# A recurrence with an MLP on one core: N in a second tile ahead of the join, GpSimd's conversions ahead of the third inverse, the first two inverses on ScalarE's queue

## The chip, the cores and the metric

The kernel runs on one core of a Trainium2 chip. The metric is device time in microseconds (us). A timed figure is the median of the fast runs named beside it; a span is the profiled execution alone.

## The reference, cut to what matters

```python
# r, k, v, w, a, b: [4, 8, 768, 40] float32
for t in range(768):
    y[:, :, t] = einsum('bhd,bhde->bhe', r_t, state)
    Sa = einsum('bhde,bhe->bhd', state, a_t)
    state = state * w_t - outer(Sa, b_t) + outer(v_t, k_t)
x = y as [3072, 320]
out = gelu_exact(x @ w_in) @ w_out          # w_in [320, 2048], w_out [2048, 320], float64 inputs
```

The kernel cuts the 768 steps into 12 chunks of 64. In each chunk the recurrence becomes products of small matrices, among them the inverse of a triangular matrix.

## The kernel before

A chunk's inverse is made from N on GpSimd, in two halves of 32 columns. It goes through DRAM (store, fetch), and its off-diagonal block is joined by two rows of small products: `corner` (J from L and N) and `joined` (J2). The other rows of small products are X, RV, A, sap, saT, QY, M, av. One row is 32 calls of `mm` (`make_QY` has two rows); in the trace a row is 64 MATMUL and 64 LDWEIGHTS records, so 128 TensorE instructions. Between the rows, `fill()` puts pieces of the MLP of an earlier chunk: ph (x @ w_in, 4.6 us) and po (gelu @ w_out, 4.5 us).

```python
def store_inverse(c):                       # 2 transfers; fetch_inverse: 6
    ...
        nc.sync.dma_start(out=rows[par], in_=W[par * n:(par + 1) * n])

def corner(c):
    L = work.tile([P, 2 * G * NP, BL], FP32, tag="L", name="L")
    nc.vector.transpose(L, flat(Tt)[:, :, :BL])
    ...                                     # J <- N, L: 64 products
    nc.scalar.copy(Js, J[:, :G * NP])

for c in range(2, NCH):                     # the loop, chunks 2 to 11
    make_X(c); fill()
    ...                                     # loads of chunk n + 1
    make_RV(n); make_sa(c); fill()
    make_saT(c); make_A(n); fill()
    make_y2(c); make_M(c); fill()
    make_QY(c); outputs(c); ...
    make_av(n); sums(n + 1); scale(n + 1); ...; turn_state(); fill()
    store_inverse(n); fetch_inverse(n); turn_b(n + 1); fill()
    corner(n)
    turn_k(n + 1); make_N(n + 1); run(start_inverse(n + 1, nc.gpsimd)); fill()
    joined(n)
```

Ahead of the loop, chunks 0 to 2 are done while the weights arrive as 64-bit words and are converted to float32 on VectorE, ScalarE and GpSimd (ten pieces of w_in on GpSimd, `first_convert`; w_out on VectorE).

## Time and profile before

| | before |
|---|---|
| median of 3 runs | 841.15 us (840.09 to 844.39) |
| profiled span | 838.1 us |
| start: up to X of chunk 2 | 254.34 us |
| from there to the end | 583.8 us, 56.06 us per iteration |
| TensorE busy in that second part | 566.88 us, clock 1.00 |

The second part is nearly full (566.88 of 583.8 us). The start is a chain of waits. A wait is read as "engine, what it was about to compute, whose result ended the wait: us in total, times, longest". The lines are in the prediction.

### The profile page before, as it was taken

The page shows a single profiled execution, that of the slowest core. Times are in us where ns is not written, and L with a number is a line of the kernel's source. Part 1 is how long each engine was busy: PE and PEld are TensorE (multiplying, and loading weights), DVE is VectorE, ACT ScalarE, POOL GpSimd, SP SyncE. Part 2 cuts the span into 40 slices and gives each one's busy share as a digit, 9 for nine tenths or more (in the row PEclk, how much of TensorE's full clock was granted, in tenths as well). Part 3 has the DMA queues.
Part 4 walks back from the last instruction along what each step waited for, and adds up shares of the span by engine and source line. Part 5 has one row for each costly group of instructions (what it writes and reads, how often), then busy time and mean ns, then how long its engine had stood idle before and what let it go on. Part 6 is the DMA issues. An engine that isn't in the chain of part 4 may idle for free.

```text
span 838.1 us, 30219 instructions
## 1 busy us (share of the span) xinstructions
PE 702.7 (84%) x13646; PEld 563.3 (67%) x13646; DVE 279.1 (33%) x422; ACT 214.0 (26%) x260; POOL 315.2 (38%) x781
## 2 busy tenths in 40 slices
PE   7236771165669999999999999999999999999997
PEld 4226661054448878778788787787887877868785
DVE  3763440147542422432424324324233243211000
ACT  5002540212312412422323124223232242111010
POOL 4282336620105507418246074182461751810000
PEclk8555595575859999999999999999999999999999
DMA  9876743017617247354372473543724733020000
GB/s 132 158 156 130 147 112 89 0 40 155 142 34 140 43 82 130 60 103 80 64 135 50 84 135 55 109 77 68 129 57 76 142 55 65 4 53 10 25 9 16
DMA packets 274705, 70.27 MB, mean 84 GB/s; under 512 B 263248, under 2 KB 267856, under 8 KB 274576
## 3 DMA queue, kind: packets, MB, share of 16 engines
q1 hardware_dynamic: 274412, 68.17, 42.6%
q8 instruction: 107, 1.75, 0.9%
q14 instruction: 22, 0.18, 0.1%
q10 hardware_dynamic: 164, 0.16, 0.1%
HBM read 54.13 MB, written 10.22 MB: 77 GB/s over the span
## 4 chain that ended last, share of the span: by engine, by line
PE 73%; POOL 6%; DMA 6%; issue 5%; SPq 4%; DVE 4%; ACT 0%; POOLq 0%; DVEq 0%
PE ph L726 25%; PE po L734 24%; PE QY L100 5%; PE J L100 2%; PE N_ps L100 2%; DMA w_out_sb<-in_moe_w_in_dram 2%; PE cum L100 2%; PE M_ps L100 1%; POOL W L548 1%; POOL mant L281 1%; PE sap L100 1%; POOL tmp L546 1%; PE saT_ps L100 1%; PE X L100 1%; PE wT_ps L100 1%
## 5 line engine op out<-in xcount | busy, mean ns | idle before, releaser
L726 PE MATMUL ph<-xt,w_in_sb 64*128 64x256 f32 x1920 | 225.8, 388 | 42.2 <-ACT gt L728 29.8
L734 PE MATMUL po<-w_out_sb,gt 128*128 128x320 f32 x768 | 225.7, 448 | 9.1 <-DVE w_out_sb L277 8.0
L726 PEld LDWEIGHTS ph<-xt,w_in_sb 64*128 64x128 f32 x1920 | 185.7, 190 | 68.0 <-ACT gt L728 30.2
L734 PEld LDWEIGHTS po<-w_out_sb,gt 128*128 128x128 f32 x768 | 145.9, 195 | 72.2 <-DVE w_out_sb L277 12.4
L546 POOL TENSOR_TENSOR tmp<-W,Nb 128x126 f32<-128x126 f32 (+22 forms) x310 | 111.8, 361 | 213.2 <-DMA Nb<-N 189.7
L548 POOL TENSOR_TENSOR W<-W,tmp 128x126 f32<-128x126 f32 (+22 forms) x310 | 113.9, 368 | 24.3
L728 ACT ACTIVATE gt<-ph 128x1024 f32<-128x1024 f32 x48 | 49.1, 1024 | 232.5 <-PE ph L726 197.5
L738 DVE COPY os<-po 128x320 f32<-128x320 f32 x24 | 11.8, 492 | 152.5 <-PE po L734 152.5
L413 POOL TENSOR_TENSOR ks<-k_raw,part 128x640 f32<-128x640 f32 x10 | 21.2, 2119 | 100.5 <-ACT part L378 85.1
L100 PE MATMUL RV_ps<-rT,vT 40*64 40x64 f32 x768 | 16.4, 244 | 30.8 <-DVE rT L166 30.8
L100 PEld LDWEIGHTS RV_ps<-rT,vT 40*64 40x64 f32 x768 | 14.7, 156 | 34.5 <-issue 34.5
L686 DVE TENSOR_TENSOR xt<-QY,wpT 128x512 f32<-128x512 f32 x24 | 15.5, 686 | 65.5 <-PE QY L100 65.5
L464 DVE TENSOR_TENSOR SM<-M_ps,upper 128x1024 f32<-128x1024 f32 x12 | 14.7, 1224 | 65.7 <-PE M_ps L100 65.7
L464 DVE TENSOR_TENSOR A<-A_ps,upper 128x1024 f32<-128x1024 f32 x12 | 14.7, 1221 | 54.6 <-PE A_ps L100 54.6
L520 ACT COPY avs<-av 128x640 f32<-128x640 f32 x12 | 8.3, 692 | 90.4 <-PE av L100 51.8
L464 DVE TENSOR_TENSOR VR<-RV_ps,upper 128x1024 f32<-128x1024 f32 x12 | 14.7, 1225 | 47.7 <-PE RV_ps L100 47.7
L100 PE MATMUL J<-L,N 32*32 32x32 f32 x768 | 9.9, 204 | 23.9 <-DVE L L585 23.9
L270 ACT ACTIVATE power<-power,rebias 128x320 uint32<-128x320 uint32 (+1 forms) x26 | 16.0, 623 | 51.6 <-DVE power L269 51.6
L100 PEld LDWEIGHTS J<-L,N 32*32 32x32 f32 x768 | 8.9, 116 | 29.4 <-issue 29.4
L464 DVE TENSOR_TENSOR N<-N_ps,upper 128x1024 f32<-128x1024 f32 x12 | 14.7, 1225 | 36.0 <-PE N_ps L100 36.0
L424 DVE TENSOR_TENSOR aT<-aT,wpT 128x1024 f32<-128x1024 f32 x12 | 24.0, 2001 | 1.6 <-ACT wpT L380 0.4
L728 ACT ACT_TABLE_LOAD x10 | 12.8, 1283 | 42.6 <-PE ph L726 40.1
(133 smaller groups left out, 869.0 us busy)
## 6 DMA issues: line engine op xcount, KB each, us to landing
Nb<-N SPq DMA_DIRECT2D x22, 256.0 KB
VR<-in_v_dram SPq DMA_DIRECT2D x24, 160.0 KB
out_dram<-os SPq DMA_DIRECT2D x48, 80.0 KB
w_tile<-in_w_dram SPq DMA_DIRECT2D x22, 160.0 KB
b_raw<-in_b_dram SPq DMA_DIRECT2D x22, 160.0 KB
k_raw<-in_k_dram SPq DMA_DIRECT2D x22, 160.0 KB
v_pairs<-in_v_dram SPq DMA_DIRECT2D x48, 72.0 KB
r_pairs<-in_r_dram SPq DMA_DIRECT2D x48, 72.0 KB
```

The source lines that it names most:

```text
L100: nc.tensor.matmul(o, lhsT, rhs, start=first, stop=True, skip_group_check=True)
L270: nc.scalar.activation(power, power, ACT.Relu, bias=rebias, scale=8.0)
L413: nc.gpsimd.tensor_tensor(ks[:, :, :, :D], raws.pop((c, "k")), rwv, ALU.mult)
L424: nc.vector.tensor_tensor(flat_a, flat_a, wp, ALU.mult)
L464: nc.vector.tensor_tensor(to, pt, upper.unsqueeze(1).to_broadcast([P, 2 * G * NP, C]), ALU.mult)
L546: eng.tensor_tensor(t, W[:, :rows, j:j + 1].to_broadcast([P, rows, rest]), Nb[:, j:j + 1, j + 1:].to_broadcast([P, rows, rest]), ALU.mult)
L548: eng.tensor_tensor(W[:, :rows, j + 1:], W[:, :rows, j + 1:], t, ALU.add)
L686: nc.vector.tensor_tensor(xt[:, :NP, g * P:(g + 1) * P].rearrange("p i (e t) -> p i e t", e=2), Y, wp[:, g, :, :, :C], ALU.mult)
L726: nc.tensor.matmul(ph[:, x, s], w_in_sb[half(x), kt, p * P:(p + 1) * P], xt[half(x), kt], start=kt == 0, stop=kt == NK - 1)
L728: nc.scalar.activation(gt[:, 4 * q:4 * q + 4].rearrange("p (x s) t -> p x s t", x=2), ph, ACT.Gelu)
L734: nc.tensor.matmul(po[:, g], gt[:, f, g * P:(g + 1) * P], w_out_sb[:, f], start=f == 0, stop=f == NF - 1)
L738: nc.vector.tensor_copy(os, po[:, g])
```

## The change

Three intents: the first inverses should not queue behind SyncE's loads; GpSimd's conversions should not wait behind the third inverse; and N of the chunk after next, in a second tile, should no longer wait for the corner, so that the join can move behind X. Its core:

```diff
-        N = t["N"] = work.tile(..., tag="turned" if c == 1 else "N", name="N")
+        if c > 1 and c % 2:
+            N = work.tile([P, 4 * DM], FP32, tag="spare", name="N")[:, :2 * G * NP * C]
+        else:
+            N = work.tile(..., tag="turned" if c == 1 else "N", name="N")
...
-    def store_inverse(c):
+    def store_inverse(c, eng=nc.sync):      # fetch_inverse alike
...                                          # the start
-    first_load(True, 0, early(4))
     run(inverse)
-    store_inverse(0)
     turn_v(0)
     turn_r(0)
+    store_inverse(0, nc.scalar)
+    load_VR(1)
+    fetch_inverse(0, nc.scalar)
...
+    store_inverse(1, nc.scalar)
...
+    fetch_inverse(1, nc.scalar)
...
     make_N(2)
+    convert(3, True)
     run(start_inverse(2, nc.gpsimd))
...                                          # the loop, n2 = c + 2
+        corner(c)
         make_X(c)
         fill()
         if more2:
-            load_next(n + 1)
+            load_next(n2)
+        joined(c)
         if more:
             make_RV(n)
+            make_A(n)
+        fill()
         make_sa(c)
-        fill()
         make_saT(c)
-        if more:
-            make_A(n)
         fill()
...
-        if more:
-            corner(n)
         if more2:
-            turn_k(n + 1)
-            make_N(n + 1)
-            run(start_inverse(n + 1, nc.gpsimd))
+            make_N(n2)
+            run(start_inverse(n2, nc.gpsimd))
+            turn_k(n2)
         fill()
-        if more:
-            joined(n)
```

More of the change, by code (lines that the diff above doesn't have):

```diff
@@ L203 @@
     ahead = {n: t.rearrange("p (g h d) -> p g h d", g=G, h=H) for n, t in ahead.items()}
-    spare_raw = const.tile([P, 4 * DM], UINT32, name="spare_raw")
+    spare_raw = work.tile([P, 4 * DM], UINT32, tag="spare", name="spare_raw")
     early_a = spare_raw.bitcast(FP32).rearrange("p (n d) -> p n d", d=BW)
@@ L487, in make_N @@
         t = turned_in[c]
-        N = t["N"] = work.tile([P, 2, G, NP, C], FP32, tag="turned" if c == 1 else "N", name="N")
+        if c > 1 and c % 2:
+            N = work.tile([P, 4 * DM], FP32, tag="spare", name="N")[:, :2 * G * NP * C]
+            N = N.rearrange("p (j g n t) -> p j g n t", j=2, g=G, n=NP)
+        else:
+            N = work.tile([P, 2, G, NP, C], FP32, tag="turned" if c == 1 else "N", name="N")
+        t["N"] = N
         masked(flat(N), products("N_ps", t["nT"], t["aT"], True))
@@ L559, in store_inverse, with fetch_inverse @@
         for par in range(2):
-            nc.sync.dma_start(out=rows[par], in_=W[par * n:(par + 1) * n])
+            eng.dma_start(out=rows[par], in_=W[par * n:(par + 1) * n])
         stored[c] = inv
-    def fetch_inverse(c):
+    def fetch_inverse(c, eng=nc.sync):
         inv = stored.pop(c)
@@ L569, in fetch_inverse @@
                 at = j * HP + z * BL
-                nc.sync.dma_start(out=flat(Tt)[at:at + BL, :, z * BL:(z + 1) * BL],
+                eng.dma_start(out=flat(Tt)[at:at + BL, :, z * BL:(z + 1) * BL],
                                   in_=inv[j, z].rearrange("n s t -> s n t"))
         for j in range(2):
-            nc.sync.dma_start(out=T2[j * HP:j * HP + BL], in_=inv[j, 1].rearrange("(n z) s t -> z s n t", z=2)[1])
+            eng.dma_start(out=T2[j * HP:j * HP + BL], in_=inv[j, 1].rearrange("(n z) s t -> z s n t", z=2)[1])
         inverses[c] = Tt, T2
@@ L812 @@
     first_load(False, 1)
-    first_load(True, 0, early(4))
     run(inverse)
-    store_inverse(0)
     turn_v(0)
     turn_r(0)
+    store_inverse(0, nc.scalar)
+    load_VR(1)
+    fetch_inverse(0, nc.scalar)
+    first_load(True, 0, early(4))
+    load_v(1)
     mask_A(0)
@@ L821 @@
     turn_k(1)
+    corner(0)
     make_A(1, False)
-    load_VR(1)
-    fetch_inverse(0)
-    load_v(1)
-    first_load(False, 2, early(5, 4))
-    first_pieces(range(NK), 0, nc.gpsimd)
+    joined(0)
     mask_A(1)
-    corner(0)
-    joined(0)
     make_X(0)
     make_sa(0)
-    convert(1)
-    store_inverse(1)
+    make_saT(0)
+    first_pieces(range(NK), 0, nc.gpsimd)
+    store_inverse(1, nc.scalar)
     nc.gpsimd.memset(spare_st.rearrange("p e i g d -> p (e i g) d")[:, :, D:], 0.0)
     load_r(1)
-    load_w(2)
-    make_saT(0)
     convert(1)
-    fetch_inverse(1)
     make_y2(0)
     make_M(0)
-    convert(1)
+    fetch_inverse(1, nc.scalar)
+    load_w(2)
     load_a(2)
     load_kb(2)
-    logs(2)
-    first_load(False, 3)
+    first_load(False, 2, early(5, 4))
+    convert(2)
     make_QY(0)
@@ L850 @@
     pieces.append(mlp(0))
+    first_load(False, 3)
     first_load(True, 1, spare_raw[:, :LW])
@@ L860 @@
     make_X(1)
+    logs(2)
     convert(1)
@@ L866 @@
     make_sa(1)
-    scale(2)
+    scale_b(2)
     turn_a(2)
     scale_a(2)
+    make_saT(1)
     convert(1)
-    make_saT(1)
     turn_b(2)
+    scale_k(2)
     convert(1)
@@ L877 @@
     make_N(2)
+    convert(3, True)
     run(start_inverse(2, nc.gpsimd))
-    convert(1)
+    second_load(4, 6)
+    second_load(5, 2, spare_raw)
+    second_load(6, 0, spare_raw)
     fill()
+    second_pieces((*range(NF - 2), NF - 1, NF - 2), nc.vector)
     make_y2(1)
     make_M(1)
-    convert(1)
+    seconds(2, (7, 14))
+    fill()
     load_v(2)
     load_r(2)
-    turn_k(2)
-    convert(1, True)
-    second_load(4, 6)
-    fill()
-    second_pieces((*range(NF - 2), NF - 1, NF - 2), nc.vector)
-    seconds(2, (5, 2, spare_raw), (6, 0, spare_raw))
-    fill()
     make_QY(1)
     outputs(1)
+    pieces.append(mlp(1))
+    seconds(2, (8, 12), (9, 10))
     load_VR(3)
-    pieces.append(mlp(1))
-    seconds(3, (7, 14), (8, 12))
-    load_w(3)
-    load_a(3)
-    load_kb(3)
+    fill()
+    turn_k(2)
     turn_v(2)
@@ L905 @@
     make_A(2)
+    load_w(3)
+    load_a(3)
+    load_kb(3)
+    seconds(3)
+    seconds(2, (10, 2, spare_raw), (11, 0, spare_raw), (12, 14))
+    fill()
     make_av(2)
-    seconds(2, (9, 10))
+    logs(3)
     load_v(3)
     load_r(3)
-    seconds(2, (10, 2, spare_raw), (11, 0, spare_raw))
-    fill()
-    logs(3)
-    seconds(2, (12, 14))
     sums(3)
-    store_inverse(2)
-    fetch_inverse(2)
     scale(3)
@@ L919 @@
     scale_a(3)
-    seconds(2, (13, 2, spare_raw), (14, 0, spare_raw))
+    seconds(2)
     turn_state()
     fill()
-    seconds(1, (15, 14))
+    seconds(2, (13, 2, spare_raw))
+    store_inverse(2)
+    fetch_inverse(2)
     turn_b(3)
+    seconds(1, (14, 0, spare_raw), (15, 14))
     seconds(2, last=True)
     fill()
-    corner(2)
-    turns_b(3)
     make_N(3)
     run(start_inverse(3, nc.gpsimd))
+    turns_b(3)
     fill()
-    joined(2)
     for c in range(2, NCH):
-        n = c + 1
-        more, more2 = n < NCH, n + 1 < NCH
+        n, n2 = c + 1, c + 2
+        more, more2 = n < NCH, n2 < NCH
+        corner(c)
         make_X(c)
@@ L939 @@
         if more2:
-            load_next(n + 1)
+            load_next(n2)
+        joined(c)
         if more:
             make_RV(n)
+            make_A(n)
+        fill()
         make_sa(c)
-        fill()
         make_saT(c)
-        if more:
-            make_A(n)
         fill()
@@ L952 @@
         if more2:
-            logs(n + 1)
+            logs(n2)
         make_QY(c)
@@ L957 @@
         if more2:
-            load_VR(n + 1)
-            turn_a(n + 1)
-            turn_v(n + 1)
-            turn_r(n + 1)
+            load_VR(n2)
+            turn_a(n2)
+            turn_v(n2)
+            turn_r(n2)
         fill()
@@ L965 @@
         if more2:
-            sums(n + 1)
-            scale(n + 1)
-            scale_a(n + 1)
+            sums(n2)
+            scale(n2)
+            scale_a(n2)
         if more:
@@ L975 @@
         if more2:
-            turn_b(n + 1)
+            turn_b(n2)
         fill()
-        if more:
-            corner(n)
         if more2:
-            turn_k(n + 1)
-            make_N(n + 1)
-            run(start_inverse(n + 1, nc.gpsimd))
+            make_N(n2)
+            run(start_inverse(n2, nc.gpsimd))
+            turn_k(n2)
         fill()
-        if more:
-            joined(n)
     fill(1000)
```

## The prediction

> **What bounds the kernel now.** I read the engine totals first, then the slices, then a table of stretches, then TensorE's waits, and last the timeline around the longest wait. The slices say where time is lost:
>
> ```profile
> PE   7236771165669999999999999999999999999997
> ...
> POOL 4282336620105507418246074182461751810000
> ...
> PEclk8555595575859999999999999999999999999999
> ```
>
> One slice is 21 us. TensorE is full from slice 13 on; before that it is half empty and mostly at a lowered clock, and slices 7 and 8 are nearly empty. The stretches put numbers on it (us busy and instructions per engine, granted clock, DMA share, GB/s):
>
> ```profile
> 105.00:127.50 22.50, 16.45 (x336) 14.08 (x327) 10.19 (x15) 9.57 (x14) 7.02 (x8) 0.92 0.45 119
> 127.50:159.60 32.10, 1.81 (x8) 1.41 (x8) 0.45 (x1) 1.02 (x1) 24.47 (x64) 0.51 0.21 48
> 159.60:185.00 25.40, 16.44 (x208) 12.33 (x208) 8.64 (x16) 8.49 (x13) 7.84 (x7) 0.68 0.08 27
> 185.00:254.34 69.34, 43.52 (x540) 29.69 (x540) 42.48 (x91) 16.45 (x24) 2.90 (x4) 0.68 0.49 105
> 254.34:838.00 583.66, 566.88 (x11088) 458.23 (x11080) 165.37 (x193) 146.29 (x166) 227.22 (x590) 1.00 0.40 74
> ```
>
> 254.34 us is where X of chunk 2, the loop's first product, starts. After it TensorE works 567 of 584 us at full clock: only less work could shorten that part. Before it lie 254 us that are a chain of waits. The longest, from TensorE's waits between 105 and 165 us, and its cause in the timeline:
>
> ```profile
> PE ph L726 <- ACT gt L728: 29.8, 1, 29.8
> ```
> ```profile
> 157.05 0.23 POOL L548 TENSOR_TENSOR W<-W,tmp 128x16 f32<-128x16 f32 x1
> 157.23 1.27 POOL L281 TENSOR_TENSOR mant<-mant,gt 128x512 f32<-128x512 f32 x1
> 158.54 1.02 ACT L728 ACTIVATE gt<-ph 128x1024 f32<-128x1024 f32 x1 [34.95 <-POOL mant L281]
> ...
> 159.61 2.08 PE L726 MATMUL ph<-xt,w_in_sb 64*128 64x256 f32 x8 [29.80 <-ACT gt L728]
> ```
>
> "ACT gt" is not the cause. The activation writes gt where raw words of w_in still lie, GpSimd's conversion (L281) must read those first, and GpSimd has done nothing but the third inverse since 130.3 us. The inverse holds the conversion, that the activation, that the PSUM buffer, that TensorE.
>
> [...] Here the first inverse is done at 49.2 us, but its store stands behind eight loads on the sync queue and is issued at 55.55; 6.3 us is all that ScalarE's queue can save there. [...] the 64 instructions of N_ps take 1.16 us in the loop (clock 1.00) and 1.98 us in the start, and the clock in the long wait is 0.51. So an estimate for the start must use the start's own durations. [...] The trace has 1.28 us for the load[...], so I count 1.28.
>
> **The change, part by part.** The number of instructions of each kind hardly changes (ten conversions on GpSimd, sixteen on VectorE, eleven inverses on GpSimd, one on VectorE); order and queues do. I followed each engine's new instruction order by hand with durations of the trace.
>
> *1. The first two inverses on ScalarE's queue.* Before:
>
> ```profile
> 43.85 11.60 SPq L325 DMA_DIRECT2D w_out_sb<-in_moe_w_in_dram  x8
> ...
> 55.55 1.97 SPq L560 DMA_DIRECT2D inv<-W  x2
> ...
> 62.90 0.71 DVE L585 STREAM_TRANSPOSE L<-Tt 128x512 f32<-128x512 f32 x1 [2.23 <-DMA Tt<-inv]
> ```
>
> After: issued at about 50, in competition with the w_in loads landed at 55 to 56, fetched by 59 to 60; L some 3.5 us earlier, and sap at about 64.5 instead of 67.8. But these issues and their waits now stand in ScalarE's program ahead of its arithmetic. The second inverse is stored after saT (about 70), landed at about 75, fetched by 77 to 79; only then can ScalarE do its part of the first conversion, so GpSimd starts it at about 79.5 to 80.5 (78.8 before). xt comes at about 83.5 (82.8). Logs(2), now after av, put an Ln with its table load (2 us) between av and cum. The fifth conversion, which the first ph waits for, starts at about 113.5 and is written at 116 (114.3). Sum of part 1: early gain given back, **+1 to +2 us** at 116.
>
> *2. Conversions ahead of the third inverse.* One conversion takes a period of 5.0 us on the ring of DVE, ScalarE and GpSimd (starts before: 157.2, 162.2, 167.2). After: ks(2) 116 to 117.6; second-half conversions start at about 118.6, 125.7 (ScalarE waits for the end of the first ph and loads its table), 130.7, 135.6, and the last, overlapped, at 138.2, ending at **140.8** (before 172.4: 31.6 earlier). TensorE does both first ph, N and M until about 129, idles until 139 to 141, then the rest of the third ph, QY (3 us) and the fourth ph: end at about **152**, against 181.4 for the fourth ph and 184.3 for QY before: 32 us earlier. The idle of 30 becomes one of 10 to 12.
>
> *3. The third inverse later.* It starts at 141 instead of 130 and ends after its 27 us at about **168**. It is needed only by the store ahead of chunk 2, at 216.5 us before and about 190 in the new order. It lies beside other work.
>
> *4. Second weights and the join.* From RV(2) the order of work is much as before: before, RV(2) starts at 195.5, last conversion ends at 238.6, X(2) starts at 254.3, 58.8 us in all. After: outputs(1) on VectorE to 151, two conversions (1.93 us each), two transposes, RV(2) at about 157, masks to 162, five conversions to 172; then av, Ln, cum, Exp, nb, aT (12 us in which VectorE converts nothing), from 184 four conversions to 192; store and fetch of the inverse to 197; the loads of the last two pieces behind it on the sync queue, landed at 201; last conversion ends at 206.5 to 209. Then the rest of po (2 us), N and kT (3.9), po (6.4, as at 247.3 before, clock recovering), os, L and J (2.5): X(2) at **221 to 224**, 30 to 33 us earlier. (The length from RV(2) is then 64 to 67, some 6 us more than before: the corner comes later, and the last two loads wait for the fetch.)
>
> *5. N ahead of the join, second tile.* N(c+2) no longer waits for the corner to have read N(c+1). But in the loop GpSimd has slack (it waits 179.5 us in all for Nb), and TensorE's only loop wait stays:
>
> ```profile
> 357.23 0.49 DVE L738 COPY os<-po 128x320 f32<-128x320 f32 x1 [6.22 <-PE po L734]
> 357.64 0.70 DVE L585 STREAM_TRANSPOSE L<-Tt 128x512 f32<-128x512 f32 x1
> ...
> 358.49 0.74 PE L100 MATMUL J<-L,N 32*32 32x32 f32 x64 [1.29 <-DVE L L585]
> ```
>
> In the new order L again follows an os on VectorE, and J again follows that po on TensorE: 1.29 us per chunk as before. The second ph of a chunk now needs the first's activation: its end comes 2.4 us after ph (ph ends 316.0, activation 318.47), while J2, RV and A fill 2.8 us. Just enough. An iteration stays at 56.06 us. From X(2) to the end: 583.7 plus one join (0.7) that moved behind X: 584.4.
>
> **Sum.** 221 to 224 plus 584.4 is 805 to 808.5 us of span; the timed median lies 3 us above the profiled span (841.15 against 838.1): 808 to 811.5. I take **810 us**.
>
> **Rivals.** (a) ScalarE's queue hurts: if the inverse's small pieces (64 KB writes in rows of 128 bytes) get half of the DMA engines, ScalarE's arithmetic waits longer, each us of it in the conversions' path. The DMA share is 0.70 between 50 and 105 us, so 5 to 8 us are possible: 815 to 818. (b) The second weights bind, not the inverse: VectorE is busy 42.5 of the 69 us from 185 on, and the sync queue carries the last loads behind the inverse; if a spare half comes free late, the gain shrinks by 5 to 10: 815 to 820. If those loads land early, X(2) could come at 216: 803. (c) The loop: if J's wait vanished, 9 times 1.29, 11.6 us more gain, 798; if ph waited for the activation (table load included), up to 1 us per chunk, 820. For (c) I see nothing in the order that removes the wait. (d) The stall merely moves: TensorE waits for the late inverse instead. Against it speaks 168 versus about 190.
>
> **Range and chances.** My errors are sums of hand-followed waits, some 6 us either way, wider on the slow side for contention: 799 to 822 should hold it 8 times in 10. The limit of 2% faster is 824.3: faster 0.95, same 0.04, slower 0.01.
>
> **What would show it.** Right: GpSimd's ten conversions end near 141 and the inverse's columns run 142 to 169; the wait of 29.8 is gone with some 10 us of waits for w_in_sb in its place; X(2) starts at 221 to 224; iterations stay at 56.06 with 1.29 us before each J; first L near 59.5, yet the first conversion no earlier than 79. Wrong: X(2) after 232 or before 215, a loop iteration off by over 0.5 us, or TensorE waiting for L because the third inverse was fetched late.

## The result

The changed kernel takes **856.07 us** (median of 4 runs, 854.54 to 857.22) against 842.77 (4 runs, 840.09 to 845.93) of the kernel before on the same chip: ratio 1.0155, 95% interval 1.0112 to 1.0199, so slower, but by less than 2%. Ratios are the mean time of one kernel's fast runs over that of the other's of the same rounds, so they are not quite the ratio of the medians. 810 was predicted, with a range of 799 to 822. The span is 855.5 us.

The slices of the profile after, one digit for each of 40 equal slices of the span, for TensorE, GpSimd and TensorE's granted clock:

```profile
PE   6206366647489989989999999899899999999997
POOL 4381224771036146154173182361541832700000
PEclk9556677766688989999999999999999999999999
```

The hole of slices 7 and 8 has gone, but TensorE is no fuller than before in slices 1 to 12, and in the loop some slices now show 8. The table of stretches (us, then busy us and instructions of TensorE, its weight loads, VectorE, ScalarE, GpSimd; clock; DMA share; GB/s) puts both losses into numbers:

```profile
183.90:245.05 61.15, 41.30 (x477) 26.53 (x477) 34.45 (x74) 15.29 (x21) 9.10 (x22) 0.68 0.51 99
245.05:855.50 610.45, 582.62 (x11152) 470.31 (x11144) 165.26 (x193) 145.68 (x167) 224.38 (x590) 0.97 0.37 70
```

X of chunk 2 starts at 245.05 us: 9.3 us earlier than before, where some 30 to 33 were predicted. From there the kernel needs 610.45 us instead of 583.8, where 584.4 were predicted. Two separate losses, then.

**The start.** TensorE's waits between 30 and 255 us, after:

```profile
PE RV_ps L100 <- DVE rT L166: 40.6, 2, 29.8
PE po L740 <- DVE w_out_sb L277: 15.7, 9, 6.9
PE J L100 <- DVE L L591: 15.2, 2, 14.0
PE ph L732 <- POOL w_in_sb L282: 9.3, 1, 9.3
```

The same view of the kernel before has this for RV:

```profile
PE RV_ps L100 <- DVE rT L166: 30.8, 2, 19.7
```

The wait of 29.8 us for ScalarE's gt has shrunk to one of 9.0 (not among the lines above), and a wait of 9.3 us for w_in_sb has come, where some 10 us for w_in_sb alone were predicted. But RV of chunk 0 now waits 10 us longer for rT, the transposed r, and J waits 14.0 us for L. The timeline shows where r was (start, us it took to issue, SyncE's queue), before:

```profile
34.74 4.34 SPq L158 DMA_DIRECT2D r_pairs<-in_r_dram  x8
```

and after:

```profile
35.37 23.39 SPq L158 DMA_DIRECT2D r_pairs<-in_r_dram  x8
...
61.00 1.25 DVE L166 STREAM_TRANSPOSE rT<-r_pairs 128x1024 f32<-128x1024 f32 x1 [10.07 <-DMA r_pairs<-in_r_dram]
```

The waits of SyncE's queue name what it stood for:

```profile
SPq L158 <- DMA Tt<-inv: 19.7, 2, 18.7
```

A load of r waited 18.7 us until the first inverse had been fetched, with which it has nothing to do in the program. Everything behind it on SyncE's queue came late.

**The loop.** TensorE's waits between 255 and 760 us, after:

```profile
PE J L100 <- DVE L L591: 10.4, 8, 1.3
PE A_ps L100 <- issue: 10.3, 8, 2.4
```

The kernel before has in the same window only its J wait:

```profile
PE J L100 <- DVE L L585: 11.6, 9, 1.3
```

"issue" is time in which nothing that the profile shows held the engine. The timeline of one iteration, after, around such a place:

```profile
312.55 1.16 PE L100 MATMUL RV_ps<-rT,vT 40*64 40x64 f32 x64
313.53 0.52 PE L100 MATMUL A_ps<-aT,kT 40*64 40x64 f32 x23
316.45 1.35 PE L100 MATMUL A_ps<-aT,kT 40*64 40x64 f32 x41 [2.40 <-issue]
317.73 6.90 PE L732 MATMUL ph<-xt,w_in_sb 64*128 64x256 f32 x40
```

A_ps stops after 23 of its 64 products, although the program has a wait only in front of the first. And the ph behind it takes 6.90 us instead of 4.59: the clock granted is 0.50 from 315.63 to 322.45 us, 0.66 on average over this ph, where it is 1.00 over the whole loop of the kernel before. The iterations (X to X) last 61.23, 61.36, 59.16, 58.94, 58.14, 59.42, 57.22 and 56.88 us instead of 56.06.

### The profile page after: what moved, and what is told of

The parts are those of the page before. It is cut to its first block, busy times and chain, and to the rows that moved or that the text cites.

```text
span 855.5 us, 30268 instructions
## 1 busy us (share of the span) xinstructions
PE 710.2 (83%) x13646; PEld 569.0 (67%) x13646; DVE 283.1 (33%) x422; ACT 213.7 (25%) x260; POOL 314.7 (37%) x781
## 3 DMA queue, kind: packets, MB, share of 16 engines
q8 instruction: 107, 1.75, 0.9%
## 4 chain that ended last, share of the span: by engine, by line
PE 70%; issue 10%; SPq 5%; DVE 5%; DMA 4%; POOL 4%; ACT 1%; ACTq 0%; POOLq 0%; DVEq 0%
PE ph L732 25%; PE po L740 22%; PE QY L100 5%; PE J L100 2%; PE A_ps L100 2%; SPq L158 2%; PE RV_ps L100 2%; PE cum L100 1%; PE sap L100 1%; PE N_ps L100 1%; PE saT_ps L100 1%; POOL mant L281 1%; PE X L100 1%; PE wT_ps L100 1%; PE kT_ps L388 1%
## 5 line engine op out<-in xcount | busy, mean ns | idle before, releaser
L732 PE MATMUL ph<-xt,w_in_sb 64*128 64x256 f32 x1920 | 236.4, 402 | 18.4 <-POOL w_in_sb L282 9.3
L740 PE MATMUL po<-w_out_sb,gt 128*128 128x320 f32 x768 | 223.9, 444 | 17.4 <-DVE w_out_sb L277 15.7
L732 PEld LDWEIGHTS ph<-xt,w_in_sb 64*128 64x128 f32 x1920 | 194.7, 199 | 45.3 <-POOL w_in_sb L282 9.9
L740 PEld LDWEIGHTS po<-w_out_sb,gt 128*128 128x128 f32 x768 | 144.0, 193 | 80.9 <-DVE w_out_sb L277 22.8
L614 DVE COPY Tt<-J 32x512 f32<-32x512 f32 x12 | 8.3, 689 | 75.6 <-ACT Tt L614 75.6
L100 PE MATMUL A_ps<-aT,kT 40*64 40x64 f32 x768 | 19.2, 249 | 15.3 <-issue 13.8
L100 PEld LDWEIGHTS A_ps<-aT,kT 40*64 40x64 f32 x768 | 16.8, 160 | 17.0 <-issue 14.9
L442 ACT COPY kT<-kT_ps 128x1024 f32<-128x1024 f32 x12 | 12.1, 1012 | 58.7 <-PE kT_ps L388 58.7
L641 DVE COPY SM<-sap 128x640 f32<-128x640 f32 x12 | 9.9, 825 | 50.6 <-PE sap L100 50.6
```

The costliest lines, as they stand in the source:

```text
L100: nc.tensor.matmul(o, lhsT, rhs, start=first, stop=True, skip_group_check=True)
L442: nc.scalar.copy(kT, flip(by_pair(t["ks"]), "kT_ps"))
L732: nc.tensor.matmul(ph[:, x, s], w_in_sb[half(x), kt, p * P:(p + 1) * P], xt[half(x), kt], start=kt == 0, stop=kt == NK - 1)
L740: nc.tensor.matmul(po[:, g], gt[:, f, g * P:(g + 1) * P], w_out_sb[:, f], start=f == 0, stop=f == NF - 1)
```

## The experiments

In the diffs, "start" is everything ahead of the loop. Sixteen kernels ran in four batches; all were correct. The kernel before took 843.29, 840.83, 841.06 and 841.11 us (medians of 7) beside them.

### Taking the two losses apart

**sync**: the changed kernel, with the first two inverses back on SyncE's queue.

```diff
-    store_inverse(0, nc.scalar)
+    store_inverse(0)
-    fetch_inverse(0, nc.scalar)
+    fetch_inverse(0)
...                                  # the same for inverse 1
```

> The changed kernel with the first two inverses back on SyncE's queue; everything else of the change stays. Theory: the start's loss comes from the two queues sharing completion semaphores, so that r_pairs' load waited on SyncE's queue for the inverse's fetch. Then r_pairs is issued in 4 to 5 us instead of 23.4, RV of chunk 0 starts near 52 instead of 62, the conversions on GpSimd end near 141 to 146 instead of 161, X of chunk 2 starts at 221 to 228 instead of 245, and the loop stays as slow as in the changed kernel (610 us from X of chunk 2 to the end): 831 to 840 us in all, 16 to 24 below the changed kernel. Rival: the order of the conversions and the second weights ate the start's gain, the queue is innocent; then X of chunk 2 stays at 240 or later and the total at 850 or more.

Measured: 837.93 us, ratio 0.9915 (0.9866 to 0.9965). The loads of r and X of chunk 2, in its timeline:

```profile
33.99 4.52 SPq L158 DMA_DIRECT2D r_pairs<-in_r_dram  x8
...
226.88 1.14 PE L100 MATMUL X<-st,aT 40*64 40x40 f32 x64
```

The theory holds: RV of chunk 0 starts at 51.8 us; GpSimd's last conversion starts its second step at 138.9 us and takes 1.27, so it ends at 140.2, just ahead of the 141 to 146 expected; and the loop stays slow (839.7 minus 226.88 is 612.8 us).

**loopb**: the changed kernel with the loop of before; `corner(2)` and `joined(2)` are back at the end of the start.

```diff
-        corner(c)
         make_X(c)
...                                  # all of the loop's part of the change undone
```

> The changed kernel with the loop of the kernel before (one tile order for N, the corner and the join at the end of an iteration); the start stays as changed, ScalarE's queue included. Theory: the order of the loop, not the start or the second tile, costs the 26 us after X of chunk 2. Then X of chunk 2 stays near 245, the iterations are 56.1 us again, no stall in the middle of A_ps, and the total is 829 to 835. Rival: the loop lost its time to something that the start left behind (a clock, the state of the tiles); then it stays at 850 or more.

Measured: 833.14 us (0.9875; 0.9831 to 0.992). X of chunk 2 stays at 244.97, seven of its eight full iterations last 56.06 us (the other 57.65), and A_ps does not stall. The theory holds.

**startb**: the start of before, the second tile for N, the changed loop.

```diff
-    store_inverse(0, nc.scalar)
...                                  # all of the start's part of the change undone
```

> The kernel before with only the loop changed (second tile for N, N ahead of the join, the products in the changed order); its start and its queues are those of before. Theory: the loop's order alone costs 25 to 27 us: X of chunk 2 at 254 to 256, A_ps stalls of 1 to 2.5 us in the middle of its products in the early iterations, total 864 to 872, 3% slower than before. Rival: the loop's loss comes from the changed start; then this is 838 to 845.

Measured: 865.3 us (1.0249; 1.0202 to 1.0296). X of chunk 2 came at 249.1, a little earlier than I expected; A_ps stalls seven times. The changed loop alone is slower.

**sync_loopb**: both undone.

> The changed start with the inverses on SyncE's queue, and the loop of the kernel before. Theory: both losses are gone and the gain that was predicted for the start (30 us) appears: X of chunk 2 at 221 to 228, iterations of 56.1 us, total 806 to 816. Rival (the start's gain is eaten by the second weights): X of chunk 2 at 240 or later, total 826 or more.

Measured: 815.51 us (0.9665; 0.9617 to 0.9712), X of chunk 2 at 231.56, later than the 221 to 228 expected and 4.7 us later than in `sync`. The join of chunk 2 (0.7 us) stands ahead of X here and behind it in `sync`; the rest is not explained and may be scatter between executions: `before` and `before_A`, whose starts are the same, have this X at 254.34 and 259.76. Differences of some 5 us in one profile's start are therefore not read as effects. With both losses out, the time is 5.5 us above the 810 that was predicted for the whole change.

### The start: how one queue held the other

**act0** keeps only the first inverse on ScalarE's queue, **act1** only the second.

```diff
 act0:                                   act1:
-    store_inverse(1, nc.scalar)         -    store_inverse(0, nc.scalar)
+    store_inverse(1)                    +    store_inverse(0)
...                                      # fetch_inverse alike
```

> The changed kernel with only the first inverse's store and fetch on ScalarE's queue; the second is back on SyncE's. Theory of shared completion semaphores: the load of r_pairs, built between the two, still has to wait for that inverse's fetch: issued over about 23 us as in the changed kernel, X of chunk 2 near 243 to 247, total 850 to 858. Rival: the second inverse (or the load on ScalarE's program) did the harm: then r_pairs takes 4 to 5 us and the total is 833 to 842.

> The changed kernel with only the second inverse's store and fetch on ScalarE's queue; the first is back on SyncE's. Theory of shared completion semaphores: the load of r_pairs has its plain turn of semaphores again and is issued in 4 to 5 us, X of chunk 2 at 225 to 232, total 833 to 842. Rival: any use of ScalarE's queue costs as much: total 850 or more.

Measured: act0 851.87 us (1.0109; 1.0051 to 1.0167), act1 837.4 (0.9977; 0.9905 to 1.0049). The loads of r in act0's timeline:

```profile
34.34 23.51 SPq L158 DMA_DIRECT2D r_pairs<-in_r_dram  x8
```

and in act1's:

```profile
35.96 4.49 SPq L158 DMA_DIRECT2D r_pairs<-in_r_dram  x8
```

It is the first inverse that costs most, not the use of ScalarE's queue as such. X of chunk 2 comes at 239.5 in act0 (I had expected 243 to 247) and at 229.2 in act1. The second inverse holds SyncE's queue too, at less cost: in the changed kernel a load of w_in waits 8.4 us for its store,

```profile
SPq L325 <- DMA inv<-st: 8.4, 1, 8.4
```

and in act1 a load of v waits 6.0 us for it:

```profile
SPq L158 <- DMA inv<-st: 7.9, 2, 6.0
```

The trace records with each transfer which semaphore it waits for and which it counts up. In the changed kernel (times on the page's clock):

```
35.37  SyncE    r_pairs, 1st of 8   waits for S109   counts up S109
36.00  SyncE    r_pairs, 2nd        waits for S101   counts up S101
53.34  ScalarE  Tt<-inv, 1st of 4   waits for S99    counts up S106
55.20  SyncE    r_pairs, 3rd        waits for S106   counts up S106
```

Eight semaphores (101 and 104 to 110) serve the transfers of both queues in turn. The third load of r is to use S106 after the inverse's fetch, so it waits until that has landed: the fetch's last update of S106 is at 55.18 us, r is issued at 55.20. In `sync`, `act1` and the kernel before, the eight loads of r use 105 to 110, 101, 104 in plain turn, and no transfer of the inverse stands between them. The trace gives the number as an operand of the transfer's instruction. In the changed kernel the numbers fit one turn over both queues merged: eight loads of v with the inverse's two stores among them, then the last two loads of N, Tt, r and T2 mixed (105 N, 106 Tt, 107 N, 108 Tt, 109 r, 110 Tt, 101 r, 104 Tt, 105 T2, 106 r). This is not the order of the program, where the loads of r stand ahead of the inverse's store and fetch (so act0's "built between the two" is not right for the loads of chunk 0). Why the turn runs so is not shown.

### The loop: what stops A_ps

The first theory was that three rows of small products behind one another (J2, RV, A: 384 instructions) outrun TensorE's instruction stream.

**startb_rv**: RV out of that place.

```diff
-            make_RV(n)
             make_A(n)
...
             turn_b(n2)
+            make_RV(n2)
```

> The kernel of run startb (start of before, changed loop) with RV of the next chunk moved from between J2 and A_ps to just ahead of N, so that no three runs of small products stand behind one another. Theory: the stall in A_ps is TensorE's instruction stream not coming fast enough[...]. Then the stall is gone, the iterations are 56 to 57 us, and the total is 838 to 848. Rival: A_ps stalls for another reason (its operands, a DMA); then it still stalls and the total stays at 858 or more.

**startb_loads**: the loads elsewhere.

```diff
-        if more2:
-            load_next(n2)
         joined(c)
...
         make_saT(c)
+        if more2:
+            load_next(n2)
```

> The kernel of run startb with the loads of the chunk after next moved from before J2 to after saT; J2, RV and A_ps stay in a row. Theory (instruction stream): stalls and total stay, 858 to 870. Rival: the loads collide with the J2, RV, A stretch and make the stall; then the stall is gone and the total falls to 838 to 848.

**before_A**: in the kernel before, A moved behind RV, so that RV, A and sap stand in a row. (The expectation names J2; in fact X and ph stand between J2 and RV there.)

```diff
             make_RV(n)
+            make_A(n)
...
-        if more:
-            make_A(n)
```

> The kernel before with one move: A_ps of the next chunk right behind RV in the loop, as in the changed kernel, and nothing else of the change. Now J2, RV and A_ps stand in a row. Theory (instruction stream): stalls in A_ps appear here too, each some 2 us with a lowered clock behind it, 2 to 3 us per iteration in all; total 855 to 870. Rival: the cost lies in N ahead of the join or in the second tile; then this stays at 840 to 846.

Measured: startb_rv 864.69 us (1.0254; 1.0189 to 1.0319), startb_loads 867.6 (1.0327; 1.0276 to 1.0379), before_A 843.89 (1.0022; 0.9981 to 1.0064). The loads are innocent. But the theory fell in this form: startb_rv still stalled, now inside ph, three times (5.1 us in the profile, which is of the fastest of its four executions), and before_A has three rows in a row without any stall.

The next theory came out of the raw trace. The page of the changed kernel lists a queue of instructions whose count fits TensorE's (packets, MB, share of the DMA engines):

```profile
q8 instruction: 107, 1.75, 0.9%
```

1.75 MB over 107 is 16384 bytes a packet. The kernel has 27,481 TensorE records: 107 blocks of 256 are 27,392, so the count fits one packet for 256 instructions. Numbering TensorE's records by their start, from 0, every stall falls on the same number modulo 256:

```
changed kernel, stalls after X of chunk 2
instruction   modulo 256   stopped   packet landed before it goes on
 5569         193          2.12 us   1.64 us
 7873         193          2.40      1.29
10177         193          1.30      1.40
12481         193          1.08      1.55
14785         193          0.33      1.26
17089         193          1.58      1.72
19393         193          0.87      1.67
21697         193          0.67      1.37
```

In the eighteen kernels there are 92 such stalls of over 0.25 us after X of chunk 2, all at 193 modulo 256, each 1.2 to 1.8 us after a packet has landed; the other gaps there are waits for semaphores, at any number. In the second part of the kernel before, the packets start between 4.6 us ahead of and 2.2 us behind such a number, one packet for each. The reading that fits: 193 is a block's edge, and TensorE stops there when the next block has come too late. The next two runs move the edges without touching the order.

**sync_64** and **sync_256**: tiny products in the warm-up at the very start, results unread.

```diff
         mm(pt[:, n % 2], w_in_sb[:, 0, :P], w_in_sb[:, 0, :512])
+    for n in range(32):                 # sync_256: 128
+        mm(pt[:BL, 0, :BL], w_in_sb[:BL, 0, :BL], w_in_sb[:BL, 0, BL:2 * BL])
```

> Run sync with 32 tiny products (64 TensorE instructions, results unread) added right at the start of the program, where TensorE is idle; nothing else. In the runs so far every stall in the loop falls on a TensorE instruction whose number is 193 modulo 256, 1.2 to 1.8 us after a packet of the instruction queue has landed. Theory: instructions come in blocks of 256, and the stall depends on where the block boundary falls, not on the order as such. 64 more instructions move the boundary from A_ps back into RV, with the boundary before it in ph. Then the stalls vanish or shrink below 0.5 us, iterations are near 56.1 us, total 810 to 818. Rival: the row J2, RV, A_ps as such is too dense, or A_ps waits for data; then 32 dummies change nothing: 833 to 842.

> The control of run sync_64: 128 tiny products, 256 TensorE instructions, one whole block. Theory: the boundary is back in A_ps, the stalls are back as in run sync (0.5 to 2.5 us each, at 193 modulo 256 again): total 833 to 842. Rival: the dummies act in another way (a warmer clock at the start, a shift in time); then this is like run sync_64 or better.

Measured: sync_64 842.92 us (1.0002; 0.994 to 1.0064), sync_256 847.61 (1.0077; 1.0019 to 1.0135). The first is a miss in two ways. Each tiny product is four TensorE instructions, not two (27,611 records against 27,483), so the shift was 128 and not 64; and the stalls did not vanish: eight of nine moved out of A_ps (two into X, two into the ph behind X, four into the ph behind A), still at 193 modulo 256. sync_256 shifted by 512, two whole blocks, and the stalls are back in A_ps in eight of nine cases. It is slower than `sync` because its X of chunk 2 comes at 235.1 instead of 226.9: the longer warm-up delayed the start (RV of chunk 0 starts at 61.2 us instead of 51.8).

With that, the question became whether the changed order is worse in itself or only met the edges badly. **beforeA_p128** and **before_p128** put the same 32 products (128 instructions) into before_A and into the kernel before; **sync_p64** puts 16 (64 instructions) into `sync`; **fill_p128** is told further down.

> Run before_A (RV, A and sap in a row, no stall at 843.9 us) with 32 tiny products, 128 TensorE instructions, at the start. If the phase decides: the boundary moves from A_ps + 57 to RV + 57, the block behind it is RV's rest, A and the head of sap, 2.0 us of work, and sap stalls by 1 to 2.5 us in every iteration: 858 to 872 us. If the order as such decides (J2 ahead of RV and A): no stalls, 840 to 848.

> The kernel before with the same 128 instructions at the start. Its densest rows are two runs of products (256 instructions) with ph or po between them. If two in a row are safe in most phases: no stall over 1 us, 839 to 849. If the kernel before was only lucky in its phase: stalls as in run sync, 855 or more.

> Run sync with 16 tiny products, 64 TensorE instructions. The boundaries move from A_ps + 42 to RV + 106, from J2 + 42 to the last fifth of ph, from X + 3 to the middle of J. If the phase decides alone, this is the best one for the changed loop that I find: stalls near 1 us in RV or A or none, total 815 to 832. If the changed order is too dense in any phase: stalls of over 1.5 us somewhere in each iteration, 833 or more.

Measured: beforeA_p128 877.57 us (median of 3 fast runs, a fourth was slow; 1.0414, 1.0339 to 1.049), before_p128 846.93 (1.0075; 1.0027 to 1.0122), sync_p64 835.41 (0.9948; 0.9908 to 0.9988). Two of these are misses in size: beforeA_p128 is slower than the 858 to 872 expected, and sync_p64 lies above its 815 to 832, with stalls of 0.5 to 1.7 us. before_A's timeline has the row without a gap:

```profile
321.41 1.16 PE L100 MATMUL RV_ps<-rT,vT 40*64 40x64 f32 x64
322.39 1.11 PE L100 MATMUL A_ps<-aT,kT 40*64 40x64 f32 x64
323.33 1.09 PE L100 MATMUL sap<-part,Tt 64*64 64x40 f32 x64
324.35 4.59 PE L726 MATMUL ph<-xt,w_in_sb 64*128 64x256 f32 x40
```

In beforeA_p128 the same row stops inside sap, where it was expected:

```profile
321.20 1.16 PE L100 MATMUL RV_ps<-rT,vT 40*64 40x64 f32 x64
322.18 1.11 PE L100 MATMUL A_ps<-aT,kT 40*64 40x64 f32 x64
323.11 0.63 PE L100 MATMUL sap<-part,Tt 64*64 64x40 f32 x29
325.68 1.28 PE L100 MATMUL sap<-part,Tt 64*64 64x40 f32 x35 [1.94 <-issue]
326.90 7.18 PE L726 MATMUL ph<-xt,w_in_sb 64*128 64x256 f32 x40
```

128 unread instructions at the start cost 34 us here: nine stalls of 19.3 us together, and the clock, at half for 27.3 us around them. So the place of the edges decided whether this dense row stalled. But order matters too. In the kernel before, where never more than two rows stand together, the same shift brings six stalls of 3.5 us in all. In the changed loop none of the four phases (places of the edges) tried is free of stalls (8.8 us in `sync`, 14.8, 10.2 and 8.4 us in sync_64, sync_256 and sync_p64).

### A version that beats both

**sync_fill**: sync_loopb, with L transposed first and N and kT of the chunk after next (second tile) put ahead of J in one run. RV and A stay apart, as before.

```diff
         if more:
-            corner(n)
+            turn_L(n)                   # the transpose of L alone
         if more2:
-            turn_k(n + 1)
             make_N(n + 1)
             run(start_inverse(n + 1, nc.gpsimd))
+            turn_k(n + 1)
+        if more:
+            corner(n)
         fill()
```

> The start of run sync_loopb, and the loop of before with N of the chunk after next ahead of J in the same run (second tile) and L transposed first, and RV and A apart as before. Theory: N and kT fill J's wait of 1.29 us per iteration and no stall appears: iterations near 55 us, 8 to 12 us below sync_loopb (815.5), total 803 to 809. Rival: the wait moves to another place in the loop or a stall appears; then it stays at 813 or more.

> Run sync_fill with the same 128 instructions at the start. If its rows of products are short enough in any phase: 803 to 812. If it was lucky: stalls of 1 to 3 us per iteration and 820 or more.

Measured: sync_fill **805.68 us** (0.9566; 0.953 to 0.9602), fill_p128 807.06 (0.9597; 0.9569 to 0.9625). J no longer waits in sync_fill's loop:

```profile
332.27 1.16 PE L100 MATMUL N_ps<-aT,nT 40*64 40x64 f32 x64
333.36 1.09 PE L388 MATMUL kT_ps<-ident,ks 128*128 128x128 f32 x8
334.38 0.75 PE L100 MATMUL J<-L,N 32*32 32x32 f32 x64
```

Six of its eight full iterations last 54.71 us, 1.35 less than 56.06. One stall of 0.4 us appears when the edges are shifted by 128, so the time holds in both phases tried. This is where the second tile pays: N has to stand *in front of J, in the same run*, while VectorE does L.

## Why the prediction was wrong, point by point

1. **"+1 to +2 us" for the first two inverses on ScalarE's queue: this step failed.** It measured 18.2 us at X of chunk 2 (245.05 against 226.88 in `sync`); the first inverse alone makes 12.6 of them (act0, 239.51), the second alone 2.3 (act1, 229.17), which is within the scatter told above. The arithmetic of issue times was right, since the fetch was indeed issued early (53.34 us), but the step took the two queues as independent, an assumption that no trace had shown. A load of r waited 18.7 us on SyncE's queue for a semaphore that the inverse's fetch counts up. The step reckoned with issue time alone, 6.3 us to be saved; the move cost three times that. Rival (a) named the right change but the wrong cause (contention in the DMA engines) and 5 to 8 us; its size of the inverse's writes was off too (each store is 128 KB, not 64).
2. **"ending with 140.8" for the conversions: right, once step 1 is taken out.** `sync` has 140.2; the changed kernel has 161.2, carrying the late start. The idle of 29.8 us gave way to waits of 9.3 and 9.0 us (the second for gt); in `sync` they are 2.6 and 9.0, together the 10 to 12 predicted.
3. **The third inverse "beside other work": right.** In `sync` it runs from 140.1 to 170.0, and no wait for it shows before the loop.
4. **"X(2) at 221 to 224": right within 3 to 6 us, once step 1 is out.** `sync` has 226.88. RV(2) came at 163.9 where I had 157; the 63 us from there to X(2) were estimated as 64 to 67.
5. **"An iteration stays at 56.06 us": this step failed, and by the larger amount.** From X(2) to the end it took 610.45 us, not 584.4. The working looked at waits between engines, where J's 1.29 us did stay, and at the activation's 2.4 us. It counted J2, RV and A as 2.8 us of work that fits. It did not ask whether 384 instructions arrive in 2.8 us. In the stall of the table's second line, the edge before it (instruction 7617, at 312.05 us) lay in J2, the packet of the next block started 1.95 us behind that, took 1.16, and TensorE went on 1.29 later: 4.4 us for a block of about 2.0 us of work. Of the 26.7 us more than before, the stalls themselves are 10.3; 15.7 are longer TensorE busy time (582.62 against 566.88, of which 0.7 is the join that moved into this part), and in seven stretches of 3.4 or 6.8 us, 30.7 us in all, the clock was at 0.50, which alone would account for about 15 us (an estimate: half of 30.7). Four of them (20.5 us) begin during a stall or up to 1.5 us behind one, the other three (10.2 us) 1.3 to 2.3 us behind J's wait. Rival (c) looked for up to 1 us per chunk in another wait. The prediction's opening sentence that "only less work could shorten that part" was wrong as well: `sync_fill` has the same products from X of chunk 2 on and needs 573.6 us for them, 10.2 less than before.
6. **The offset of 3 us** between span and median was 0.6 (855.5 and 856.07). The 3 us compared different executions: an execution's time stands 1.7 us above its own span, before (839.78 and 838.1) as after (857.22 and 855.5).

The errors add up: about 21 to 24 us in the start, 26 in the loop, minus 2.4, which is the 46 us between 810 and 856. What stays open: why the block behind an edge in J2 is fetched 1.9 to 2.7 us ahead of that edge in the loop of the kernel before (po stands in front of J2), but between 0.3 us ahead of it and 1.95 us behind it in the changed one (ph stands there). The two differ in density, po with 32 instructions in 4.5 us and ph with 80 in 4.6; whether that is the reason is not shown. Nor is it separated which gaps go with a halved clock: in the kernel before, with J's wait of up to 1.3 us in each iteration, the clock stays at 1.00 from 251.09 to 838.19 us; beside J's wait alone stands one halved stretch in loopb (its iteration of 57.65 us) and three in the changed kernel. All seven stretches there begin on one grid of 3.413 us (18, 36, 51, 68, 88 and 136 steps behind the first); whether a gap's place on that grid matters, no run tests.

## What to carry to other kernels

Moving a transfer to another engine's queue tied the first queue to it here, by 18.7 us: look in the profile at how long *unrelated* transfers now take to issue. To have them earlier in the program was not enough; the loads of r stood ahead of the inverse's store and were still caught. Count instructions as well as time where many small products stand in a row: here rows of 384 instructions at 5 to 9 ns each stalled by 0.3 to 2.4 us in the changed kernel, and a shift by 64 or 128 instructions moved the stalls. A buffer that removes a dependency is of use where an engine really waits: here the second tile brought an iteration from 56.06 to 54.71 us only when the freed work stood directly in front of J.
